# Windowed attention with its gradients: quads of four tiles below one another, merged stores, and x loads issued by GpSimd

## The chip, the cores and the metric

The kernel runs on one core of one Trainium2 chip. A core has five engines that run side by side and wait for one another by semaphores: TensorE (matmuls; PE in the profile, its weight loads PEld), VectorE (DVE), ScalarE (ACT), GpSimd (POOL) and SyncE (SP). Sixteen DMA engines move data between HBM and the on-chip memory (SBUF), and within SBUF; SyncE and GpSimd issue nearly all of those transfers here. TensorE writes its results to PSUM, which has eight banks. The metric is the device time of one execution in microseconds; lower is better.

## What is computed

The input x is an image of 256 x 256 pixels with 384 channels (bf16). It is cut into windows of 8 x 8 pixels, 1024 in all; each window is a sequence of 64 tokens. Within a window there is attention with one head, then an output projection. The kernel returns this output and, for a given grad_out, the gradients of x, wqkv and wo.

```python
xw = x in windows                                  # 1024 x 64 x 384
q, k, v = split(xw @ wqkv)
p = softmax(einsum('bqc,bkc->bqk', q, k) * C ** -0.5)
o = einsum('bqk,bkc->bqc', p, v) @ wo              # out_0, back in image order
out_1, out_2, out_3 = vjp of the above at (x, wqkv, wo), applied to grad_out
```

## The kernel before

**Products folded ahead.** Lines 61 to 107 load the weights once and make four 384 x 384 matrices of them, with wq, wk and wv the three column blocks of wqkv: A and its transpose AT from wq and wk with the scale in them, B and its transpose BT from wv and wo. So the loop never makes q, k and v. Per tile it makes y (x by A, L165) and z (grad_out by BT, L163), from which come scores and the gradients of p, and u = x B and v = x AT (L231).

**Tiles and quads.** A tile is 128 tokens: two windows, one below the other (16 image rows of 8 pixels); its lower 64 partitions (LO) hold one window, the upper 64 (HI) the other. A quad is four tiles. Before the change the four tiles of a quad lie side by side (`t0` to `t0 + 3` in the band `bp` of 16 rows, L349), so there are 128 quads.

**Steps.** The loop (L360) runs one step a quad, with three quads in work at once (L309): `a` (quad i+1) is projected, `b` (quad i) gets scores and softmax, `c` (quad i-1) gets its outputs. On each engine, instructions run in the order in which the program records them, without a scheduler (L353). A step on TensorE, in order: `sd` (scores of b, L177), u and v of b (L228 to L231), z of a (`project` kind 0, needs `dT`), a part of the weight gradient (`filler`, `pg`, every quad's share is summed later over groups of three quads), `attend` for tiles 0 and 1 of c, y of a (kind 1, needs `xT`), `filler`, `attend` for tiles 2 and 3 of c.

**What SyncE issues**, per step and in this order: `dT` and `xT` of quad i+2 (transposes of the loaded gradient and x, L130), `PS` of quad i (transpose of the probabilities and their gradient, L235, once VectorE's and ScalarE's parts of `ps` are done), four loads of x for quad i+3 (L120), and `tok` of quad i+1 (transposes y and z back to tokens, L169, once ScalarE has copied them out). Buffers: `xq` 10, `dq` 6, `xT` 3, `dT` 2, `PS` 2, `tok` 3.

**What GpSimd issues**: four loads of grad_out for quad i+3 (L121) between the stores of `attend` (L245). Its DMAs take turns on eight semaphores, and each waits until the DMA eight before it has landed.

**attend** (L247) works on a pair of tiles. For each tile it makes four results in a PSUM bank each: `po` (the output), `pu` and `pw` (for the weight gradients; VectorE copies them to `Uq` and `Wq`) and `pd` (the gradient of x; part of it comes from `tok`, in `token_part`). The pair uses all eight banks once. The matmuls are 64 x 64; in a "straight" one (`pu`, `pw`) a window stays in its half of the partitions, in a "crossed" one (`po`, `pd`) the window in LO comes out in HI and the other way round. ScalarE copies `po` and `pd` to SBUF (`keep`, L264); the pools for these copies have 8 buffers, two quads' worth for each output. As the halves are swapped, each copy leaves by two stores of 64 partitions (`store`, L243), so 16 stores a quad, 2048 in all.

Of the kernel before, what the change touches and what calls it, by code (L numbers as in the profile page):

```python
# [11 lines left out]
BF16 = mybir.dt.bfloat16  # L12
F32 = mybir.dt.float32

P = 128
WIN = 8
# [6 lines left out]
def kernel(  # L23
# [23 lines left out]
    CK = C // P  # L47
    J = 3 * C
    JK = J // P
    NBP = H // (2 * WIN)  # L50
    NT = W // WIN
    scale = float(C) ** -0.5

    const = ctx.enter_context(tc.tile_pool(name="const", bufs=1))
# [51 lines left out]
    GF_acc = const.tile([P, 2, CK, C], F32)  # L106
    nc.vector.memset(GF_acc[:], 0.0)

    def dram_tile(ap, bp, t):
        return ap[0, 2 * WIN * bp:2 * WIN * (bp + 1), WIN * t:WIN * (t + 1), :]  # L110

    LO, HI = slice(0, WT), slice(WT, P)
    OTHER = {0: HI, WT: LO}

    def load(st):
        bp, t0 = st["at"]
        st["xq"] = xq = grp.tile([P, QUAD, C], BF16, tag="xq", name="xq", bufs=2 * GQ + 4)
        st["dq"] = dq = qp.tile([P, QUAD, C], BF16, tag="dq", name="dq", bufs=6)
        for t in range(QUAD):
            nc.sync.dma_start(out=xq[:, t, :], in_=dram_tile(x, bp, t0 + t))  # L120
            nc.gpsimd.dma_start(out=dq[:, t, :], in_=dram_tile(grad_out, bp, t0 + t))  # L121

    def load_turn(st):
        xq, dq = st["xq"], st["dq"]
# [115 lines left out]
            return st["PS"][h, t, int((n == "ST") == (h == LO)), :]  # L240
        return st[n][h, t, :]

    def store(dst, src, bp, t):  # L243
        for h, w in ((LO, 1), (HI, 0)):
            nc.gpsimd.dma_start(out=dram_tile(dst, bp, t)[WIN * w:WIN * (w + 1)], in_=src[h, :])  # L245

    def attend(st, pair):  # L247
        bp, t0 = st["at"]
# [3 lines left out]
        def both(straight, crossed):  # L252
            for h, o, (dst, lhs, rhs, begin, done) in ((LO, LO, straight), (LO, HI, crossed), (HI, LO, crossed),
                                                       (HI, HI, straight)):
                nc.tensor.matmul(dst[o, :], lhsT=turned(st, lhs, t, h), rhs=st[rhs][h, t, :], start=begin, stop=done)  # L255

        def token_part(t, pd, first):
            for w, o in ((0, HI), (1, LO)):
                nc.tensor.matmul(pd[o, :], lhsT=st["ps"][:, t, w, :], rhs=st["tok"][:, :, t, w, :], start=first,  # L259
                                 stop=not first)  # L260

        def keep(name, eng, dst, t, src):
            sb = ob.tile([P, C], BF16, tag=name)
            ENG[EV[eng][t]](out=sb[:], in_=src[:])  # L264
            stores.append((dst, sb, bp, t0 + t))

        stores = []
        for t in pair:
            first = t == pair[0]
            po, pu = [ring.tile([P, C], F32, tag="r", name=n) for n in ("po", "pu")]  # L270
            if first:
                pd = ring.tile([P, C], F32, tag="r", name="pd")
                token_part(t, pd, True)
            both((pu, "ST", "xq", True, True), (po, "PT", "uq", True, True))
            keep("o", "o", out_0, t, po)
            ENG[EV["U"][t]](out=st["Uq"][:, t, :], in_=pu[:])  # L276
            pw = ring.tile([P, C], F32, tag="r", name="pw")
            if not first:
                pd = ring.tile([P, C], F32, tag="r", name="pd")
            both((pw, "Pb", "dq", True, True), (pd, "ST", "vq", not first, first))  # L280
            ENG[EV["W"][t]](out=st["Wq"][:, t, :], in_=pw[:])  # L281
            if not first:
                token_part(t, pd, False)
            keep("d", "d", out_1, t, pd)
        for s in stores:
            store(*s)

    fill = []

# [19 lines left out]
    def step(c, b, a, ahead):  # L309


        def on(st):
            return (lambda f, *r: f(st, *r)) if st is not None else (lambda f, *r: None)
        C_, B, A = on(c), on(b), on(a)
        B(scores)
        B(soft, 0)
        B(uv, 0, 0)
        B(uv, 0, 1)
        B(soft, 1)
        B(uv, 1, 0)  # L320
# [12 lines left out]
        B(soft, 5)  # L333
        B(turn)
        if ahead is not None:
            load(ahead)
        filler(1)
        C_(attend, (0, 1))
        split[0] = True
        for mo in range(CK):  # L340
            A(project, 1, mo)
        A(to_tokens)
        filler(1)
        split[0] = ALL
        C_(attend, (2, 3))

    G_ON_PE = 0
    EV = {"z": "AAA", "y": "AAA", "u": "AAAA", "v": "AAAA", "o": "AAAA", "U": "DDDD", "W": "DDDD", "d": "AAAA"}
    quads = [(bp, t0) for bp in range(NBP) for t0 in range(0, NT, QUAD)]  # L349
    sts = [{"at": q, "i": i} for i, q in enumerate(quads)]  # L350
    n = len(sts)
    AHEAD = 3
    with tc.manual_schedule(engines=MANUAL):  # L353
        for i in range(min(AHEAD, n)):
            load(sts[i])
            if i < AHEAD - 1:
                load_turn(sts[i])
        held = []
# [75 lines left out]
```

## Time and profile before

| what | value |
|---|---|
| median of 13 runs | 2037.19 us (2019.41 to 2047.17) |
| the profiled execution | 2047.17 us, of which the span of its instructions is 2045.1 us |
| TensorE clock granted | 0.995 of full speed |
| 2048 stores, GpSimd's time for one | 567 ns; 5.2 us to landing (median) |
| 512 loads of grad_out, GpSimd's time for one | 550 ns; 4.2 us to landing |
| 512 loads of x, SyncE's time for one (median) | 599 ns; 4.3 us to landing |
| transposes, SyncE's time (median): tok, xT, dT, PS | 5.64, 2.88, 2.02, 1.23 us |
| transposes to landing (median): tok, xT, dT, PS | 10.5, 6.6, 6.0, 4.9 us |
| 1024 copies of po and pd on ScalarE, mean of one | 490 and 500 ns |
| HBM read and written | 101.84 MB each, 100 GB/s over the span |

The profiled execution is the slowest of the 13 runs. In the profile, "L130 SPq DMA_TRANSPOSE" is SyncE issuing a transpose from line 130: the time shown is that for which the issue holds SyncE, not that of the transfer. An entry of the waits reads: engine, tile and line that waited, after the arrow what released it, then total us, number of times, longest. TensorE's matmuls overlap in the profile, so a busy share near 100% doesn't mean that it runs at its peak; how long a step takes is better read from the starts of a matmul that comes once a quad.

### The profile page before, as it was taken

What the parts mean: (1) busy time and instruction counts of PE and PEld (TensorE: products, weight loads), DVE (VectorE), ACT (ScalarE), POOL (GpSimd) and SP (SyncE); (2) the same over time, 40 slices, a digit from 0 to 9 for tenths busy, and PEclk for the clock granted to TensorE, in tenths of its full rate; (3) what the DMA queues carried; (4) which work ended last, traced back from release to release, by engine and by line L of the source; (5) the groups of instructions that cost most, each with busy time, mean ns of one, the idle gap of its engine ahead of it and who ended that gap; (6) DMA issues with size and microseconds to landing.
All of it is one profiled execution on the core that took longest, in us unless ns stands there. A gap on an engine that the chain in (4) does not pass through costs nothing.

```text
span 2045.1 us, 53141 instructions
## 1 busy us (share of the span) xinstructions
PE 1976.9 (97%) x19418; PEld 1125.2 (55%) x19418; DVE 1319.6 (65%) x2979; ACT 1423.0 (70%) x3213; POOL 1417.6 (69%) x2566
## 2 busy tenths in 40 slices
PE   8899999999999999999999999999999999999998
PEld 4455555555555555555555555555555555555555
DVE  5566666656666666666566666666666666666666
ACT  5677777767776766777667767767766767777674
POOL 3666777677766676766767767666776767777776
PEclk9899999999999999999999999999999999999999
DMA  9999999999999999999999999999999999999994
GB/s 201 184 212 208 213 216 209 207 206 209 214 212 200 213 211 215 214 209 202 205 216 212 216 215 214 211 213 205 217 209 202 217 208 219 213 220 213 215 219 115
DMA packets 1066854, 425.97 MB, mean 208 GB/s; under 512 B 950368, under 2 KB 1041248, under 8 KB 1066592
## 3 DMA queue, kind: packets, MB, share of 16 engines
q1 hardware_dynamic: 943312, 270.60, 81.3%
q0 software_dynamic: 122880, 151.68, 31.7%
q8 instruction: 152, 2.49, 0.5%
q14 instruction: 110, 0.90, 0.1%
q10 hardware_dynamic: 400, 0.29, 0.0%
HBM read 101.84 MB, written 101.84 MB: 100 GB/s over the span
## 4 chain that ended last, share of the span: by engine, by line
PE 78%; DMA 18%; ACT 2%; issue 0%; DVE 0%; SPq 0%; ACTq 0%; POOL 0%; POOLq 0%
PE pj L149 25%; PE pj L147 12%; PE pg L147 12%; DMA dT<-dq 11%; PE pg L149 10%; DMA PS<-ps 7%; PE pd L259 6%; PE pu L255 5%; PE sd L149 4%; PE pw L255 4%; ACT uq L231 1%; ACT vq L231 1%; PE pd L255 1%; DMA dq<-in_grad_out_dram 0%; DMA xT<-xq 0%
## 5 line engine op out<-in xcount | busy, mean ns | idle before, releaser
L245 POOL DMA_DIRECT2D out_dram<-sb x2048 | 1146.3, 567 | 549.7 <-DMA out_dram<-sb 225.0
L264 ACT CAST sb<-po 128x384 bf16<-128x384 f32 x512 | 250.9, 490 | 337.9 <-PE pu L255 312.2
L298 DVE TENSOR_TENSOR GF_acc<-pg,GF_acc 128x384 f32<-128x384 f32 x258 | 143.9, 558 | 519.4 <-PE pg L147 332.4
L149 PEld LDWEIGHTS <-xT 128*128 128x128 bf16 x3072 | 291.8, 98 | 182.2
L149 PE MATMUL pj<-B_sb,xT 128*128 128x384 bf16 x1536 | 333.4, 326 | 0.0
L149 PE MATMUL pj<-AT_sb,xT 128*128 128x384 bf16 x1536 | 333.3, 326 | 0.0
L121 POOL DMA_DIRECT2D dq<-in_grad_out_dram x512 | 274.1, 550 | 63.9 <-DMA out_dram<-sb 34.2
L149 PE MATMUL pj<-dT,BT_sb 128*128 128x512 bf16 x1152 | 275.5, 385 | 35.4 <-DMA dT<-dq 34.0
L276 DVE CAST Uq<-pu 128x384 bf16<-128x384 f32 x512 | 282.9, 552 | 38.5 <-PE pu L255 33.0
L231 ACT CAST uq<-pj 128x384 bf16<-128x384 f32 x512 | 247.4, 483 | 70.9 <-PE pj L149 67.8
L281 DVE CAST Wq<-pw 128x384 bf16<-128x384 f32 x512 | 280.2, 547 | 0.0
L147 PE MATMUL pj<-xT,A_sb 128*64 128x512 bf16 x2304 | 270.6, 380 | 1.0 <-DMA xT<-xq 1.0
L264 ACT CAST sb<-pd 128x384 bf16<-128x384 f32 x512 | 256.2, 500 | 0.7 <-PE pd L259 0.3
L231 ACT CAST vq<-pj 128x384 bf16<-128x384 f32 x512 | 250.1, 488 | 2.7 <-ACT uq L231 0.3
L165 ACT CAST yz<-pj 128x512 bf16<-128x512 f32 x384 | 224.2, 603 | 10.1 <-PE pj L147 2.1
L149 PEld LDWEIGHTS <-xq 128*128 128x128 bf16 x1572 | 154.4, 98 | 116.9 <-issue 3.7
L147 PEld LDWEIGHTS <-xq 128*64 128x64 bf16 x3000 | 170.3, 110 | 86.5
L163 ACT CAST yz<-pj 128x512 bf16<-128x512 f32 x384 | 207.2, 642 | 13.1 <-PE pj L149 11.7
L209 ACT COPY ps<-Pb 64x256 bf16<-64x256 bf16 x256 | 103.2, 403 | 149.7 <-DVE Pb L206 148.2
L149 PEld LDWEIGHTS <-BT_sb 128*128 128x128 bf16 x1152 | 109.2, 99 | 173.4 <-DMA dT<-dq 55.2
L255 PE MATMUL pu<-xq,PS 64*64 64x384 bf16 x1024 | 176.0, 336 | 17.2 <-DMA PS<-ps 17.0
L147 PEld LDWEIGHTS <-A_sb 128*64 128x64 bf16 x2304 | 134.3, 110 | 96.3 <-DMA xT<-xq 1.5
(60 smaller groups left out, 2486.9 us busy)
## 6 DMA issues: line engine op xcount, KB each, us to landing
out_dram<-sb POOLq DMA_DIRECT2D x2048, 48.0 KB, 5.2
xq<-in_x_dram SPq DMA_DIRECT2D x512, 96.0 KB, 4.3
dq<-in_grad_out_dram POOLq DMA_DIRECT2D x512, 96.0 KB, 4.2
dT<-dq SPq DMA_TRANSPOSE x128, 6.0
xT<-xq SPq DMA_TRANSPOSE x128, 6.6
tok<-yz SPq DMA_TRANSPOSE x128, 10.5
PS<-ps SPq DMA_TRANSPOSE x128, 4.9
w_sb<-in_wqkv_dram SPq DMA_DIRECT2D x1, 864.0 KB, 5.5
```

The lines of the kernel that those rows point to most:

```text
L121: nc.gpsimd.dma_start(out=dq[:, t, :], in_=dram_tile(grad_out, bp, t0 + t))
L147: nc.tensor.matmul(out[h], lhsT=lhsT[:, h], rhs=rhs, start=start, stop=stop)
L149: nc.tensor.matmul(out, lhsT=lhsT, rhs=rhs, start=start, stop=stop)
L163: ENG[EV["z"][mo]](out=yz[:, mo, :, 0:4:3, :], in_=pj[:])
L165: ENG[EV["y"][mo]](out=yz[:, mo, :, 1:3, :], in_=pj[:])
L231: cp(out=dst[:, t, :], in_=pj[:])
L245: nc.gpsimd.dma_start(out=dram_tile(dst, bp, t)[WIN * w:WIN * (w + 1)], in_=src[h, :])
L255: nc.tensor.matmul(dst[o, :], lhsT=turned(st, lhs, t, h), rhs=st[rhs][h, t, :], start=begin, stop=done)
L264: ENG[EV[eng][t]](out=sb[:], in_=src[:])
L276: ENG[EV["U"][t]](out=st["Uq"][:, t, :], in_=pu[:])
L281: ENG[EV["W"][t]](out=st["Wq"][:, t, :], in_=pw[:])
L298: nc.vector.tensor_tensor(out=GF_acc[:, f, ma, :], in0=pw[:], in1=GF_acc[:, f, ma, :], op=ALU.add)
```

## The change

A quad is now four tiles below one another: 64 image rows of one column of windows (`quads`, with `at` a row and a column; `windows` takes the place of `dram_tile`). The two tiles of a pair are then neighbours: the second window of the first tile borders on the first window of the second.

In `attend` the crossed results of the pair (`po`, `pd`) go to two banks by another rule. One bank ("outer" 0) takes the two windows that border on each other, the other ("outer" 1) the first window of the first tile and the second window of the second. Both are complete only when the second tile's matmuls are done, so ScalarE's four copies of a pair come after that, `po` first. Of each output, the inner bank's copy leaves by one store of 128 partitions and 16 image rows, the outer one's by two stores of 64 partitions: 12 stores a quad.

The x loads of the loop (quads 3 to 127) are issued by GpSimd, in turn with the loads of grad_out; SyncE keeps those of the first three quads. Below, SyncE's order in a step is `dT`, `xT`, `PS`, `tok`; GpSimd's is eight loads, six stores of one pair, six of the other.

```diff
-    def load(st):
-        bp, t0 = st["at"]
+    def windows(ap, st, first, count=2):
+        row, col = st["at"]
+        return ap[0, row + WIN * first:row + WIN * (first + count), col:col + WIN, :]
...
+    def load(st, queue):
...
-            nc.sync.dma_start(out=xq[:, t, :], in_=dram_tile(x, bp, t0 + t))
-            nc.gpsimd.dma_start(out=dq[:, t, :], in_=dram_tile(grad_out, bp, t0 + t))
+            queue.dma_start(out=xq[:, t, :], in_=windows(x, st, 2 * t))
+            nc.gpsimd.dma_start(out=dq[:, t, :], in_=windows(grad_out, st, 2 * t))
...
-    def store(dst, src, bp, t):
-        for h, w in ((LO, 1), (HI, 0)):
-            nc.gpsimd.dma_start(out=dram_tile(dst, bp, t)[WIN * w:WIN * (w + 1)], in_=src[h, :])
...
+        def both(straight, crossed, t, outer, **flags):
+            for h, o, (dst, lhs, rhs), fl in ((LO, LO, straight, {}), (LO, HI, crossed, flags), (HI, LO, crossed, flags),
+                                              (HI, HI, straight, {})):
+                at = dst if dst is not crossed[0] else dst[outer if h == LO else 1 - outer]
+                nc.tensor.matmul(at[o, :], lhsT=turned(st, lhs, t, h), rhs=st[rhs][h, t, :],
+                                 **{"start": True, "stop": True, **fl})
+
+        def token_part(t, pd, outer, **flags):
             for w, o in ((0, HI), (1, LO)):
...
+                nc.tensor.matmul(pd[outer if w == 0 else 1 - outer][o, :], lhsT=st["ps"][:, t, w, :],
+                                 rhs=st["tok"][:, :, t, w, :], **flags)
+
+        def keep(name, dst, src):
+            for outer in (0, 1):
+                sb = ob.tile([P, C], BF16, tag=name, name=name)
+                nc.scalar.copy(out=sb[:], in_=src[outer][:])
+                stores.append((dst, sb, outer))
+
+        t0, t1 = pair
         stores = []
...
+        pu = [bank("pu")]
+        po = [bank("po") for outer in (0, 1)]
+        pd = [bank("pd") for outer in (0, 1)]
+        token_part(t0, pd, 1, start=True, stop=False)
+        both((pu[0], "ST", "xq"), (po, "PT", "uq"), t0, 1)
+        nc.vector.tensor_copy(out=st["Uq"][:, t0, :], in_=pu[0][:])
+        pw = [bank("pw")]
+        both((pw[0], "Pb", "dq"), (pd, "ST", "vq"), t0, 1, start=False, stop=True)
+        nc.vector.tensor_copy(out=st["Wq"][:, t0, :], in_=pw[0][:])
+        pu.append(bank("pu"))
+        both((pu[1], "ST", "xq"), (po, "PT", "uq"), t1, 0)
+        keep("o", out_0, po)
+        nc.vector.tensor_copy(out=st["Uq"][:, t1, :], in_=pu[1][:])
+        pw.append(bank("pw"))
+        both((pw[1], "Pb", "dq"), (pd, "ST", "vq"), t1, 0, start=True, stop=False)
+        nc.vector.tensor_copy(out=st["Wq"][:, t1, :], in_=pw[1][:])
+        token_part(t1, pd, 0, start=False, stop=True)
+        keep("d", out_1, pd)
+        for dst, sb, outer in stores:
+            if outer:
+                nc.gpsimd.dma_start(out=windows(dst, st, 2 * t1 + 1, 1), in_=sb[LO, :])
+                nc.gpsimd.dma_start(out=windows(dst, st, 2 * t0, 1), in_=sb[HI, :])
+            else:
+                nc.gpsimd.dma_start(out=windows(dst, st, 2 * t0 + 1), in_=sb[:])
...
-            load(ahead)
+            load(ahead, nc.gpsimd)
...
-    quads = [(bp, t0) for bp in range(NBP) for t0 in range(0, NT, QUAD)]
+    quads = [(row, col) for row in range(0, H, 2 * WIN * QUAD) for col in range(0, W, WIN)]
...
-            load(sts[i])
+            load(sts[i], nc.sync)
```

More of the change, by code (lines that the diff above doesn't have):

```diff
@@ L49 @@
     JK = J // P
-    NBP = H // (2 * WIN)
-    NT = W // WIN
     scale = float(C) ** -0.5
@@ L107 @@
     nc.vector.memset(GF_acc[:], 0.0)
-    def dram_tile(ap, bp, t):
-        return ap[0, 2 * WIN * bp:2 * WIN * (bp + 1), WIN * t:WIN * (t + 1), :]
+    def windows(ap, st, first, count=2):
+        row, col = st["at"]
+        return ap[0, row + WIN * first:row + WIN * (first + count), col:col + WIN, :]
     LO, HI = slice(0, WT), slice(WT, P)
     OTHER = {0: HI, WT: LO}
-    def load(st):
-        bp, t0 = st["at"]
+    def load(st, queue):
         st["xq"] = xq = grp.tile([P, QUAD, C], BF16, tag="xq", name="xq", bufs=2 * GQ + 4)
@@ L241, in turned @@
         return st[n][h, t, :]
-    def store(dst, src, bp, t):
-        for h, w in ((LO, 1), (HI, 0)):
-            nc.gpsimd.dma_start(out=dram_tile(dst, bp, t)[WIN * w:WIN * (w + 1)], in_=src[h, :])
     def attend(st, pair):
-        bp, t0 = st["at"]
         if pair[0] == 0:
@@ L251, in attend @@
             st["Wq"] = grp.tile([P, QUAD, C], BF16, tag="Wq", name="Wq")
[L252 to L257, printed above, removed]
-            for w, o in ((0, HI), (1, LO)):
-                nc.tensor.matmul(pd[o, :], lhsT=st["ps"][:, t, w, :], rhs=st["tok"][:, :, t, w, :], start=first,
-                                 stop=not first)
@@ L262, in keep @@
[L262 to L265, printed above, removed]
-        stores = []
[L268 to L284, printed above, removed]
@@ L285, in attend, with bank @@
-        for s in stores:
-            store(*s)
+        def bank(name):
+            return ring.tile([P, C], F32, tag="r", name=name)
+        def both(straight, crossed, t, outer, **flags):
[4 more added lines that the diff above has]
+                                 **{"start": True, "stop": True, **fl})
```

## The prediction

> **What bounds the kernel now.** I read the page first (busy shares, DMA line, queues), then the waits of all engines, then SyncE's own timeline in two places, and last the times of single instructions and packets in the trace.
>
> The page says that two things are nearly always busy: TensorE and the DMA engines.
>
> ```profile
> PE 1976.9 (97%) x19418; PEld 1125.2 (55%) x19418; DVE 1319.6 (65%) x2979; ACT 1423.0 (70%) x3213; POOL 1417.6 (69%) x2566
> ...
> DMA  9999999999999999999999999999999999999994
> ...
> q1 hardware_dynamic: 943312, 270.60, 81.3%
> q0 software_dynamic: 122880, 151.68, 31.7%
> ```
>
> q1 is SyncE's queue (transposes and x loads), q0 GpSimd's (gradient loads and stores). Their packets overlap, so the shares may add up to over 100%; what the reader should take is that no slice has the DMA engines below nine tenths until the end.
>
> How often does TensorE wait? One quad begins with its first `sd` matmul; 128 such starts stand in the trace, from 22.0 to 2001.9 us. Of the 124 periods from the fourth on, 65 last under 15.2 us and most of these 15.12 or 15.13: that is TensorE's own pace, with nothing to wait for. The other 59 are longer, and everything above 15.13 adds up to 68 us. That, 3.3% of the span, is all a change around the DMAs can win. The waits say what is late:
>
> ```profile
> POOL out_dram L245 <- DMA out_dram<-sb: 225.0, 161, 4.0
> ...
> PEld L149 <- DMA dT<-dq: 55.2, 54, 5.2
> PE pj L149 <- DMA dT<-dq: 34.0, 35, 4.8
> ...
> PEld L255 <- DMA PS<-ps: 24.6, 33, 3.2
> ...
> PE pu L255 <- DMA PS<-ps: 17.0, 20, 3.0
> ```
>
> The matmul rows alone give 34.0 + 17.0 = 51 us, all behind transposes that SyncE issues. Why are they late, with two and three buffers each? SyncE's timeline in mid-run (start, time in us) answers:
>
> ```profile
> 1001.03 6.41 SPq L169 DMA_TRANSPOSE tok<-yz  x1
> 1007.67 1.47 SPq L130 DMA_TRANSPOSE dT<-dq  x1
> 1009.31 3.56 SPq L130 DMA_TRANSPOSE xT<-xq  x1
> 1013.04 1.21 SPq L235 DMA_TRANSPOSE PS<-ps  x1
> 1014.30 2.51 SPq L120 DMA_DIRECT2D xq<-in_x_dram  x4
> 1016.91 6.10 SPq L169 DMA_TRANSPOSE tok<-yz  x1
> ```
>
> One round is 15.9 us (1001.03 to 1016.91) and has no hole: SyncE goes from one issue to the next. It runs a whole quad behind: in the steps I sampled, `PS(i)` is issued 16 to 22 us after quad i's first `sd`, though its operand is there after about 8; TensorE tolerates up to about 18 to 20. Compare the start, when GpSimd issues no DMA yet:
>
> ```profile
> 24.06 2.51 SPq L120 DMA_DIRECT2D xq<-in_x_dram  x4
> 26.62 4.04 SPq L169 DMA_TRANSPOSE tok<-yz  x1
> 30.83 1.41 SPq L130 DMA_TRANSPOSE dT<-dq  x1
> 32.42 1.76 SPq L130 DMA_TRANSPOSE xT<-xq  x1
> 34.29 1.50 SPq L235 DMA_TRANSPOSE PS<-ps  x1
> 35.84 2.62 SPq L120 DMA_DIRECT2D xq<-in_x_dram  x4
> ```
>
> The same round takes 11.8 us here (24.06 to 35.84), the next one 14.0. So a transpose's issue lasts as long as the DMA engines need to take it: SyncE is held by the DMA engines, not by its own decoding. An x load costs SyncE 0.6 us in both places.
>
> GpSimd is as full. From its instruction times: 20 DMAs a quad at 0.55 to 0.57 us are 11.3 us; of the rest, 484 us in all (3.8 a quad) go by until the DMA eight before has landed, since its DMAs take turns on eight semaphores. Only 4 stores of 2048 found their copy by ScalarE unfinished.
>
> **What the Trainium skill says.** "DMA: Bandwidth & Descriptors", section "Issuing engines are not separate DMA queues": moving a DMA to another issuer saves only the sequencer's time, the same 16 engines run it. The trace agrees as far as it can: 8 rows of 768 B per engine and load cost 8 x 36 ns = 288 ns in q1 and 207 + 68 = 275 ns in q0 (medians of packets). Same page, "Why a DMA increments its semaphore by 16 and not by 1": a DMA spreads over the largest number up to 16 that divides the slowest dimension of both sides, while GpSimd's DMAs report from all 16. The trace agrees: a store of 8 x 8 x 384 puts data on 8 engines (16,384 packets each of 24 B and of 8 B are fillers for the others); a 16-row store should use all 16. Same page, "Queues, rings and completion order": an engine takes turns between queues packet by packet. The trace shows turns, but long ones: from 1237.5 to 1239 almost only transposes move, from 1240 to 1240.5 almost only GpSimd's packets.
>
> **The change part by part.**
> 1. *Quads of four tiles below one another.* A load still reads 16 rows of 8 pixels; counts and bytes stay. Rows of different tiles are no longer neighbours in HBM; at 100 GB/s of HBM traffic over the span I take 0, bound -0.1 to +0.2 us a quad.
> 2. *Merged stores.* Per pair and output three stores for four: 512 of 2048 go, 512 x 567 ns = 290 us less on GpSimd. Bytes stay; the fillers and reports of 1024 half stores go. Fillers and reports have 449.6 + 181.6 + 217.3 us of packet time on 16 engines; half of the fillers and a fifth of the reports are about 290 us, /16/128 = 0.14 us a quad.
> 3. *x loads to GpSimd.* 500 of 512 (the first three quads' stay). GpSimd: 500 x 550 ns = 275 us more, so 20 DMAs a quad as before. SyncE: 4 x 0.6 = 2.4 us less a quad. In GpSimd's order the loads stand before the first pair's stores; they are needed a full quad later, when `dT` and `xT` of that quad are issued.
> 4. *Crossed outputs in two banks.* The same matmuls in the same order, 8 banks a pair as before. ScalarE's first copy waits for the second tile: in the quad at 1727 the last `d` copy of a pair then ends about 0.35 us later. ScalarE sat idle 0.41 and 1.86 us ahead of the two pairs' first copies and 0.52 us before the next `uq`, so this is covered. The next banks are needed 0.5 to 1 us after they come free. Only the second tile's `pw` now takes the bank of the weight-gradient sum that `pd` took one matmul later: 0 to 0.05 us a quad. If the cover were gone, up to 0.35 us a pair.
>
> The sum is made in the DMA engines' time per quad, because both queues push back from there. Alone, SyncE's round is (11.8 + 14.0)/2 = 12.9 us, of which 2.5 are x: 10.4 remain. The mean round is 15.6 us, so 12 load-equivalents of GpSimd traffic (4 loads, 16 half stores) add 2.7 us, 0.22 each, partly because they slip in while SyncE spends 0.6 us on an x load that needs 0.29. Afterwards there are 16 load-equivalents at 0.22 (as now) to 0.29 us (nothing slips in): 10.4 + 3.5 to 4.6 = 13.9 to 15.0 us, less 0.14. That is under TensorE's 15.13, so TensorE becomes the limit. Not by much, and single rounds vary by 1 to 3 us [...], so I leave a third of the waits: 68 x 2/3 = 45 us gone. The profiled execution took 2047.2 us and is the longest of 13; TensorE's pace being fixed, the median of 2037.2 has about 10 us less of waits, 58. Two thirds of that is 38: **2000 us** (rounded). Its own range: all waits gone 1979, with a little spread 1976; waits down by a quarter 2022.
>
> **The rivals.**
> *A. DMA engines stay the limit.* If an x load costs 0.33 us in GpSimd's queue, a round is 10.4 + 16 x 0.33 = 15.7 and nothing moves. For: the DMA line has no hole. Against: 0.29 measured. Time 2034 (the fillers' share of the waits goes).
> *B. GpSimd becomes the limit (slower).* Place: its eight semaphores. All 20 DMAs of a quad pass through, so each delay of landing counts 20/8 = 2.5 times; 4 more of them are full loads, the bytes in flight rise by a third. Landing takes 5.2 us in the mean (over its 2560 DMAs) against about 3.4 for the fastest tenth; a third more of the 1.8 us spent queueing is 0.6, of which I take half, 0.3, since q1 loses what q0 gains. 2.5 x 0.3 = 0.75 us; GpSimd has some 0.8 us a quad of other idle time, of which I let half give way; 0.35 remain, x 127 = 44 us: 2080. It decides once the mean landing rises by over 0.2 us. For: GpSimd's 14 DMAs in a row (6 stores, 8 loads). Against: SyncE's freed time leaves the DMA engines open to it.
> *C. Late copies stall TensorE (slower).* 0.1 us on 256 pairs: 26 us on top of A, 2060. Against: the idle times above.
> *D. The change doesn't do what it says:* a merged store that cost twice on GpSimd would save nothing there. The gradient load, also 128 x 384, costs 550 ns, so no; it is within B.
>
> **How the numbers follow.** Main case 0.52 (all of it faster), A 0.17, B 0.25, C 0.06. A measurement here tells about 0.5% (10 us) from no change. A lies mostly within it (0.12), a little on either side. Faster 0.55, same 0.12, slower 0.33. The range reaches from 1976 over A and C to B's 2080, leaving out half of B and little else.
>
> **What would show it.** Right: SyncE has waiting time in every round and `PS` is issued about 8 to 12 us after the quad's `sd`; TensorE's waits for `dT` and `PS` fall below 20 us; most periods are 15.13. Wrong: GpSimd's waits for its own DMAs grow from 225, the landing of stores or loads rises above 5.5 us, and SyncE or ScalarE waits for them; or ScalarE's `po` copies appear as what TensorE waits for; or SyncE is still without a hole.

## The result, and the profile after

The changed kernel takes 2269.7 us in the median (11 runs, 2248.75 to 2294.28); the kernel before took 2038.4 us beside it. The ratio is 1.113 (95% interval 1.110 to 1.117): 231 us slower, where 2000 us were forecast and the range ended at 2080. The profiled execution of the changed kernel has a span of 2246.6 us.

The page of the changed kernel, the lines that answer to those shown of before (third and last: queue, packets, MB, share of 16 engines):

```profile
PE 2042.5 (91%) x19418; PEld 1195.0 (53%) x19418; DVE 1317.6 (59%) x2979; ACT 1415.8 (63%) x3213; POOL 1384.6 (62%) x2554
...
DMA  9999999999999999999999999999999999999995
...
q1 hardware_dynamic: 871312, 221.41, 69.2%
q0 software_dynamic: 122304, 200.57, 42.0%
```

TensorE's share falls from 97% to 91%. 49 MB went from q1 to q0 as intended, and the total is the same 426 MB. But the DMA line still shows nines: the engines are as busy as before and take longer over the same bytes (189 GB/s in the mean over the span, 208 before). The two shares times the span, over 128 quads, are the time that the packets took on 16 engines: 13.0 + 5.1 = 18.1 us a quad before, 12.1 + 7.4 = 19.5 now. (Packets of two queues overlap, which is why this is more than a quad lasts.) A quad now lasts 17.2 us in the mean, against 15.6, and TensorE's own pace is nearly what it was: the shortest quads take 15.20 us (15.13 before). So the loss is waiting. The waits of the changed kernel, TensorE's matmul rows:

```profile
PE pu L253 <- DMA PS<-ps: 115.6, 71, 4.9
...
PE pj L147 <- DMA dT<-dq: 64.6, 43, 4.8
```

These are the waits of before, for the same transposes, grown from 51 to 180 us on the matmul rows. What has changed is why the transposes are late. SyncE's queue of the changed kernel:

```profile
SPq L128 <- DMA dq<-in_grad_out_dram: 419.0, 131, 7.8
```

Before, this row read:

```profile
SPq L130 <- DMA dq<-in_grad_out_dram: 25.9, 14, 4.4
```

SyncE used to run without a hole, a quad behind; now it stands and waits for loads. Its timeline in mid-run (start, time in us):

```profile
998.05 6.23 SPq L167 DMA_TRANSPOSE tok<-yz  x1
1008.71 1.52 SPq L128 DMA_TRANSPOSE dT<-dq  x1
1010.40 3.45 SPq L128 DMA_TRANSPOSE xT<-xq  x1
1014.04 1.38 SPq L233 DMA_TRANSPOSE PS<-ps  x1
1015.53 6.43 SPq L167 DMA_TRANSPOSE tok<-yz  x1
1025.14 1.77 SPq L128 DMA_TRANSPOSE dT<-dq  x1
```

From 1004.28 (the end of `tok`) to 1008.71 SyncE does nothing, and again from 1021.96 to 1025.14. GpSimd's timeline over the first of these holes shows who it waits for (in brackets: idle time before the instruction, and the engine whose event the profile saw last):

```profile
999.24 0.52 POOL L119 DMA_DIRECT2D dq<-in_grad_out_dram  x1 [0.31 <-DMA out_dram<-d]
...
1003.17 0.56 POOL L290 DMA_DIRECT2D out_dram<-d  x1
1006.28 0.54 POOL L292 DMA_DIRECT2D out_dram<-o  x1 [2.55 <-ACT yz L163]
1009.12 0.56 POOL L289 DMA_DIRECT2D out_dram<-o  x1 [2.30 <-ACT o L264]
1009.67 0.56 POOL L290 DMA_DIRECT2D out_dram<-o  x1
```

The bracket names ScalarE, but these are GpSimd's own eight places: in the trace's semaphore events, the DMA eight before the store at 1006.28 landed at 1005.73, and the one eight before the store at 1009.12 is the gradient load of 999.24, which landed at 1008.57, after 9.3 us, beside the `tok` transpose. That one late load released both engines: SyncE's `dT` at 1008.71 and GpSimd's store at 1009.12. The second hole ends in the same way (the gradient load of 1017.00 landed at 1025.02; `dT` at 1025.14). These two are not exceptions: in 119 of the 128 rounds SyncE stands before `dT`, for 505 us in all (3.9 us a quad), and each of these holes ends with the landing of a gradient load of that quad. It is a loop of three: the loads that `dT` needs are the last of GpSimd's eight, they land late while `tok` runs, and while SyncE and GpSimd both wait for them, nothing new is given to the DMA engines: in quarter-microsecond steps of the trace, fewer than 12 packets were under way for about 0.9 us a quad (under 0.4 before). The mean landing of all GpSimd DMAs went from 5.19 to 5.98 us, and GpSimd's waits for the DMA eight before, worked out from the semaphore events, from some 510 to some 710 us.

### The profile page after: what moved, and what is told of

It is laid out like the page before. It is cut to its first block, busy times and chain, and to the rows that moved or that the text cites. A ratio compares the mean times of both kernels' runs of the same rounds, so it can differ in the third digit from the quotient of the medians.

```text
span 2246.6 us, 52492 instructions
## 1 busy us (share of the span) xinstructions
PE 2042.5 (91%) x19418; PEld 1195.0 (53%) x19418; DVE 1317.6 (59%) x2979; ACT 1415.8 (63%) x3213; POOL 1384.6 (62%) x2554
## 5 line engine op out<-in xcount | busy, mean ns | idle before, releaser
L264 ACT CAST o<-po 128x384 bf16<-128x384 f32 x512 | 220.4, 482 | 543.7 <-PE pu L253 520.3
L147 PE MATMUL pj<-dT,BT_sb 128*128 128x512 bf16 x1152 | 286.7, 397 | 72.8 <-DMA dT<-dq 64.6
L118 POOL DMA_DIRECT2D xq<-in_x_dram x500 | 271.6, 543 | 60.4 <-DMA out_dram<-o 33.8
L145 PE MATMUL pj<-xT,A_sb 128*64 128x512 bf16 x2304 | 305.4, 414 | 1.2 <-DMA xT<-xq 1.2
L289 POOL DMA_DIRECT2D out_dram<-o x256 | 147.3, 575 | 231.1 <-DMA dq<-in_grad_out_dram 113.5
L292 POOL DMA_DIRECT2D out_dram<-o x256 | 139.5, 545 | 216.0 <-DMA xq<-in_x_dram 57.7
L145 PEld LDWEIGHTS <-xq 128*64 128x64 bf16 x3000 | 206.6, 111 | 54.0 <-issue 3.4
L161 ACT CAST yz<-pj 128x512 bf16<-128x512 f32 x384 | 209.3, 636 | 36.8 <-issue 19.7
L163 ACT CAST yz<-pj 128x512 bf16<-128x512 f32 x384 | 209.8, 625 | 29.7 <-PE pj L145 28.7
L264 ACT CAST d<-pd 128x384 bf16<-128x384 f32 x512 | 225.5, 504 | 0.4 <-ACT o L264 0.2
L145 PEld LDWEIGHTS <-A_sb 128*64 128x64 bf16 x2304 | 165.1, 119 | 105.8 <-issue 30.8
L274 DVE CAST Uq<-pu 128x384 bf16<-128x384 f32 x256 | 141.4, 552 | 136.3 <-PE pu L253 134.4
```

What stands on the lines that cost most here:

```text
L118: queue.dma_start(out=xq[:, t, :], in_=windows(x, st, 2 * t))
L145: nc.tensor.matmul(out[h], lhsT=lhsT[:, h], rhs=rhs, start=start, stop=stop)
L147: nc.tensor.matmul(out, lhsT=lhsT, rhs=rhs, start=start, stop=stop)
L161: ENG[EV["z"][mo]](out=yz[:, mo, :, 0:4:3, :], in_=pj[:])
L163: ENG[EV["y"][mo]](out=yz[:, mo, :, 1:3, :], in_=pj[:])
L264: nc.scalar.copy(out=sb[:], in_=src[outer][:])
```

## The experiments

Ratios are to the kernel before, run on the same chip beside each; times can differ by some 10 us between chips, so runs on different chips are best compared by ratio. Two theories lead through all of them. W: GpSimd, with its eight places, is the limit; what counts is the number of its DMAs and how long each takes to land. C: the DMA engines themselves take longer when plain DMAs run beside the transposes. In SyncE's own queue x loads stand before or behind a transpose and hardly run beside one: in the trace of e1 (below) about a tenth of their bytes moved while packets of a transpose were under way, in that of e4, with x in a queue of its own, two thirds.

The table has all runs. "Beside" is what a quad moves in queues other than SyncE's, in units of one load (96 KB; whole stores count one, half stores a half). "Landing" is the mean over GpSimd's DMAs. "Places" is DMAs a quad x landing / mean period of a quad: how many of the eight are taken in the mean. "Packets" is the packet time of the queues per quad on 16 engines, as worked out above. Period, landing, places and packets come from the one profiled execution of each; for e2 and e15 that is the longest of its runs (2442 and 2035 us), for e10 one of 2196 us.

| kernel | GpSimd DMAs a quad | beside | time us | ratio (95%) | period | landing | places | packets |
|---|---|---|---|---|---|---|---|---|
| before | 20 | 12 | 2038 | 1 | 15.59 | 5.19 | 6.7 | 18.1 |
| changed | 20 | 16 | 2269.7 | 1.113 (1.110 to 1.117) | 17.17 | 5.98 | 6.9 | 19.5 |
| e3 vertical quads only | 20 | 12 | 2024.4 | 0.999 (0.996 to 1.001) | 15.33 | 5.12 | 6.7 | 18.0 |
| e1 x back on SyncE | 16 | 12 | 2004.8 | 0.988 (0.983 to 0.993) | 15.27 | 4.59 | 4.8 | 17.7 |
| e2 only x moved, stores as before | 24 | 16 | 2414.0 | 1.188 (1.180 to 1.196) | 18.68 | 5.21 | 6.7 | 19.5 |
| e4 x on ScalarE | 16 | 16 | 2128.9 | 1.050 (1.044 to 1.057) | 16.20 | 6.83 | 6.7 | 19.6 |
| e8 half of x on GpSimd | 18 | 14 | 1993.6 | 0.979 (0.975 to 0.983) | 15.17 | 5.32 | 6.3 | 18.0 |
| e13 three of four x on GpSimd | 19 | 15 | 2050.6 | 1.005 (1.003 to 1.007) | 15.65 | 5.65 | 6.8 | 18.2 |
| e11 x on GpSimd, half of gradient on SyncE | 18 | 14 | 1995.9 | 0.977 (0.972 to 0.982) | 15.19 | 5.25 | 6.2 | 17.9 |
| e12 half of x on ScalarE | 16 | 14 | 1995.1 | 0.977 (0.973 to 0.982) | 15.18 | 5.08 | 5.4 | 18.0 |
| e15 three of four x on ScalarE | 16 | 15 | 2017.3 | 0.994 (0.991 to 0.996) | 15.49 | 6.29 | 6.5 | 18.7 |
| e10 whole stores on ScalarE | 16 | 16 | 2195.7 | no interval (2158 to 2217) | 16.75 | 7.12 | 6.8 | 20.3 |
| e9 = e1 + four tiny DMAs | 20 | 12 | 2059.6 | 1.011 (1.005 to 1.017) | 15.72 | 5.24 | 6.7 | 18.4 |
| e14 = e8 + two tiny DMAs | 20 | 14 | 2053.2 | 1.015 (1.010 to 1.019) | 15.60 | 5.28 | 6.8 | 18.1 |
| e17 loads a quad earlier | 20 | 16 | 2286.9 | 1.128 (1.122 to 1.134) | 17.38 | 6.04 | 6.9 | 19.7 |
| e18 all loads on SyncE | 12 | 8 | 2342.9 | 1.151 (1.146 to 1.156) | 17.90 | 5.07 | 3.4 | 17.5 |
| e22 = e1, first U on ScalarE | 16 | 12 | 2003.5 | 0.984 (0.980 to 0.988) | 15.25 | 4.51 | 4.7 | 17.6 |
| e16 = e8, first U on ScalarE | 18 | 14 | 1983.4 | 0.980 (0.977 to 0.984) | 15.08 | 5.32 | 6.3 | 17.9 |

### Which part of the change: e1, e2, e3

e1 is the changed kernel with one word altered:

```diff
-            load(ahead, nc.gpsimd)
+            load(ahead, nc.sync)
```

> The changed kernel with the x loads of the loop back on SyncE: GpSimd has 16 DMAs a quad (4 loads, 4 whole and 8 half stores). Theory W (GpSimd's eight semaphores): GpSimd's round is 16 x 0.56 us plus at most 3 us of waiting for its own DMAs, so it limits nothing; SyncE is full again as in the kernel before; 2015 to 2050 us, mean landing of GpSimd's DMAs at or under 5.2 us. Theory H (vertical quads or the crossed banks cost the time): 2200 us or more, since both are still in.

e2 is the kernel before with only the x loads of the loop moved, and e3 the kernel before with only the quads turned (each with what follows from it at the places of use):

```diff
-            load(ahead)
+            load(ahead, nc.gpsimd)
...
-    quads = [(bp, t0) for bp in range(NBP) for t0 in range(0, NT, QUAD)]
+    quads = [(bp, col) for bp in range(0, NBP, QUAD) for col in range(NT)]
```

> The kernel before with nothing but its x loads of the loop moved to GpSimd: 24 DMAs a quad there. Theory W: each DMA counts, so it is clearly worse than the changed kernel, whose round of 17.2 us is 11.3 us of issue and 5.5 us of waiting: 24/20 of both is 20.2 us a quad, about 2600 us. Theory D (the x bytes cost more when they pass through GpSimd's queue, however many DMAs carry the rest): the same bytes are in that queue as in the changed kernel, so 2240 to 2300 us. Theory H: 2040 us, as neither vertical quads nor banks are in.

> The kernel before with only its quads made of tiles below one another; stores, banks and queues as before. Theories W and D: no difference, 2020 to 2055 us. Theory H in its HBM part: slower by over 3%, with longer landing of loads and stores.

e1 is some 10 us faster than W allowed and far from H's 2200; e2 lies between the numbers of W and D, so neither holds as it stands. Turning the quads is worth nothing (0.999), turning them and merging the stores 1.2% (0.988), and moving the x loads costs 12.7% on top of that (1.113/0.988), or 18.8% without the merge. The whole loss is the move. In e1 GpSimd has time to spare: its greatest wait is for stores whose copy isn't made yet.

```profile
POOL out_dram L292 <- ACT o L264: 689.2, 236, 28.1
```

In the changed kernel the same row has 45.5 us: there GpSimd is late for nearly all of them.

### Leaving SyncE's queue, and entering GpSimd's: e4

```diff
-            load(ahead, nc.gpsimd)
+            load(ahead, nc.scalar)
```

> The changed kernel with the x loads of the loop issued by ScalarE, on a third queue: SyncE is relieved as in the changed kernel, GpSimd has 16 DMAs a quad. Theory W: no full server is left; SyncE has holes, TensorE's waits for dT and PS fall under 20 us, 1985 to 2015 us (ScalarE has to issue 4 x 0.6 us a quad more and has the idle time for it). Theory D: only the passage through GpSimd's queue costs, so the same here. If the DMA engines themselves are the limit whatever the queue: 2030 us or more, with SyncE still full.

This misses W's number. GpSimd issues the 16 DMAs of e1, and still e4 is 6.3% slower than e1 (1.050/0.988). Nor has SyncE got the short round: its transposes alone hold it for 15.0 us a quad with hardly a hole, where in e1 they took 11.7 and the x loads 2.7. ScalarE's new work is a small part of the loss: TensorE waits 16 us for late copies of `o` (no such wait in e1), and the time rose by 124.

The changed kernel is a further 6.0% slower (1.113/1.050), but e4 is not a stop on the way to it. In the changed kernel SyncE's transposes take 12.7 us a quad, and SyncE stands for 3.9 us more, waiting for gradient loads (5 us in the whole of e4). Where e4's loss comes from is seen on the queue lines; e1's:

```profile
q1 hardware_dynamic: 943312, 270.60, 81.5%
q0 software_dynamic: 98304, 151.39, 31.4%
```

and e4's, with ScalarE's queue as q10:

```profile
q1 hardware_dynamic: 871312, 221.41, 71.8%
q0 software_dynamic: 98304, 151.39, 34.5%
q10 hardware_dynamic: 72400, 49.48, 11.9%
```

q0 moves the same 98,304 packets and 151.39 MB in both, but takes 31.4% of 2004.6 us in one and 34.5% of 2121.5 us in the other: 4.9 and 5.7 us a quad. The x loads' own 768-byte packets take 43.9 ns each in the mean in SyncE's queue and 61.3 ns in ScalarE's (medians 36 ns in both: it is the tail that grows), 1.4 and 1.9 us a quad. The transposes' packets go from 26.8 to 28.0 ns, 11.1 to 11.7 us a quad. So the four loads add 1.9 us of packet time a quad, of which only 0.5 is theirs; the rest is what all others lose beside them. The shares of e4 add up to 118%, so packets of different queues overlap, and a packet's time is not an engine's work alone; that the engines as a whole got slower is seen in the bytes, 212 GB/s over the span in e1 and 201 in e4. The mixing itself can be counted: at least three packets of transposes and three of loads or stores are under way for about 5.2 us a quad in e1, 9.7 in e4 and 7.9 in the changed kernel. Whether it matters that e4 has a third queue, e4 alone can't tell.

### The dose: e8 and e13 on GpSimd, e12 and e15 on ScalarE, e11

e8 moves two of a quad's four x loads, e13 three:

```diff
-            queue.dma_start(out=xq[:, t, :], in_=windows(x, st, 2 * t))
+            (queue if t < 2 else nc.sync).dma_start(out=xq[:, t, :], in_=windows(x, st, 2 * t))
```

For e13 it is `t < 3`; e12 and e15 are the same two edits with `load(ahead, nc.scalar)`. e11 leaves x where the change puts it and splits the other loads:

```diff
-            nc.gpsimd.dma_start(out=dq[:, t, :], in_=windows(grad_out, st, 2 * t))
+            (nc.gpsimd if t < 2 else nc.sync).dma_start(out=dq[:, t, :], in_=windows(grad_out, st, 2 * t))
```

> The changed kernel with the x loads of tiles 0 and 1 on GpSimd and those of tiles 2 and 3 on SyncE: half the dose, GpSimd issues 18 DMAs a quad (16 with x on SyncE: 2005 us; 20 in the changed kernel: 2270 us). Theory C (transposes and plain loads that run beside each other are slow together, whatever GpSimd has to spare): the loss goes with the loads that left SyncE's queue, so about half way, 2075 to 2150 us, with the mixed part of a quad between 4.8 and 7.8 us. Theory W (GpSimd's eight DMAs in flight become the limit only once its spare time, some 5.8 us a quad with x on SyncE, is used up): two more DMAs fit, 2000 to 2030 us.

The loss is not in proportion: half the dose (0.979) is faster than none (0.988), and a little faster than W's range. W, which asks whether GpSimd still has room, said so; C, as I had it, did not, since it let the mixed time grow with the loads moved: in e8 it is only 5.6 us a quad. For the next runs W was put into a number: GpSimd had 6.7 to 6.9 of its eight places taken in the runs in which it had no spare time, so that limit allows a landing of 15.2 x 8 x 0.84 / DMAs.

> The changed kernel with the x loads of tiles 0 to 2 on GpSimd and that of tile 3 on SyncE: 19 DMAs a quad on GpSimd, between 18 (1994 us) and 20 (2270 us). Theory W says that GpSimd, when it is the limit, keeps 83 to 86% of its eight places filled (DMAs a quad x mean landing / 8 / period, in the kernel before, in the changed one and in the three other runs where it had no spare time), so that a quad of 15.2 us allows a mean landing of 15.2 x 8 x 0.84 / DMAs: 6.4 us at 16, 5.7 at 18, 5.4 at 19, 5.1 at 20. Landing was 5.32 at 18, so at 19 it is just at its limit: some loss, 2005 to 2110 us, far less than three quarters of the way to 2270. A loss in proportion to the loads moved (theory C, which the run with half of them contradicts): 2200 us.

> The changed kernel, all x loads on GpSimd as there, but the gradient loads of tiles 2 and 3 on SyncE: 18 DMAs a quad on GpSimd and the same bytes in each queue as in the run with half of the x loads moved. Theory W (number and landing of GpSimd's DMAs, whatever they carry): like that run, 1985 to 2015 us. Theory T (it is x that arrives too late when it stands in GpSimd's order beside the gradient, or the transposes wait for both): the loss stays, above 2100 us.

> The changed kernel with the x loads of tiles 0 and 1 on ScalarE and those of tiles 2 and 3 on SyncE; GpSimd issues 16 DMAs a quad. With none on ScalarE: 2005 us, landing 4.59 us; with all four: 2129 us, 6.83 us. Theory W with its limit of 6.4 us at 16 DMAs: the landing stays under it, about 5.7, no loss, 1990 to 2020 us. In proportion to the loads that leave SyncE's queue (theory C): about 2065 us.

All three came out in W's range: e13 loses 2.6% to e8, with 6.8 places taken; e11, with all x loads on GpSimd and tiles 2 and 3 of the gradient on SyncE, is like e8, so it is not x as such that may not stand there. In e12, "in proportion" (2065 us) falls as well. But e12 and e8 also leave the engines with the same work beside the transposes, so these runs can't tell number from bytes.

### Number or bytes: e9, e14, e15

e9 and e14 add DMAs of 6 KB on GpSimd (four a quad to e1, two to e8), read from x into a tile that nothing reads:

```diff
+            ti = ob.tile([WIN, C], BF16, tag="ti", name="ti")
+            nc.gpsimd.dma_start(out=ti[:], in_=windows(x, st, 2 * t, 1)[0])
```

> The changed kernel with all x loads on SyncE and, in the places where the changed kernel issues x loads on GpSimd, four DMAs of 8 rows of 768 bytes there (6 KB each in place of 98 KB), into a tile that nothing reads. GpSimd issues 20 DMAs a quad as in the changed kernel, but the bytes in its queue are those of the kernel with x on SyncE. Theory W in its simplest form (the number of DMAs on GpSimd, each 0.56 us of issue and one of eight places): most of the loss returns, 2150 us or more. Theory C (bytes that run beside transposes): close to the kernel with x on SyncE, 2000 to 2035 us, landing below 5 us.

> The run with half of the x loads moved (tiles 0 and 1 on GpSimd, 2 and 3 on SyncE, 1994 us), and in the places of the other two on GpSimd a DMA of 6 KB each that nothing reads: 20 DMAs a quad on GpSimd as in the changed kernel, but 1376 KB a quad outside SyncE's queue in place of 1573. If the number of DMAs that pass through GpSimd's eight places decides (H1), most of the changed kernel's loss comes back: above 2150 us. If the bytes beside the transposes decide (H2), little comes back: 1995 to 2025 us. If both count, each with its own share, about what four tiny DMAs cost with x on SyncE (+46 us of four, from 2005): 2020 to 2060 us.

> The changed kernel with the x loads of tiles 0 to 2 on ScalarE and that of tile 3 on SyncE: 16 DMAs a quad on GpSimd, 1475 KB a quad outside SyncE's queue, as in the run with three of four on GpSimd (19 DMAs, 2051 us). With two of four on ScalarE 1995 us, with all four 2129. H2 (bytes beside the transposes decide): 2035 to 2065 us. H1 (GpSimd's places decide; 16 DMAs allow a landing of 6.4 us): no loss, 1995 to 2015 us.

e9 and e15 fall between the pure theories, and e14 into the range where both count. Put side by side as ratios to before, by GpSimd's DMAs and by what is beside the transposes, the runs say:

| beside, in loads | 16 DMAs | 18 or 19 | 20 DMAs |
|---|---|---|---|
| 12 | 0.988 (e1) | | 1.011 (e9) |
| 14 | 0.977 (e12) | 0.979 (e8), 0.977 (e11) | 1.015 (e14) |
| 15 | 0.994 (e15) | 1.005 (e13) | |
| 16 | 1.050 (e4) | | 1.113 (changed) |

Down a column is the price of bytes, along a row that of the number; but from the second row on the 16-DMA runs have ScalarE's queue as a third one. Without it, four more DMAs of next to no bytes cost 2.3% in the first row, two more cost 3.6% in the second (e14 against e8), and at 20 DMAs the bytes of two more loads cost 9.7%. With the third queue, the two loads cost 7.5%, of which 5.7 come with the last, and 16 against 20 DMAs is 6.0% in the last row. So both causes are there, each shown with the other held, and together they cost more (12.7% from e1 to the changed kernel) than e9's 2.3% and e4's 6.3%.

They act in different ways. The mixed time is about 5.2 us a quad in e1, 5.5 in e12, 8.2 in e15 and 9.7 in e4: nearly flat up to 14 loads' worth, then steep, like the times. e9 has no more of it than e1 (4.9). There GpSimd's waits for the DMA eight before go from some 100 us to over 500, and SyncE's transposes hold it for 12.2 us a quad instead of 11.7; which of the two costs the 2.3%, and why the transposes are slower, these runs don't settle. In e14 it is as in the changed kernel: SyncE stands 216 us, waiting for gradient loads.

Both begin late because TensorE covers them: up to 14 loads' worth and 18 DMAs a quad still fits into its 15.2 us. The first two loads that leave SyncE even bring 1% (e8, e11, e12 against e1), since SyncE's round gets shorter by 1.2 us and the waits for `dT` and `PS` all but vanish.

### Rate or lateness: e17. A third queue: e10

e17 issues all loads one quad earlier, with one more buffer for each:

```diff
-            step(get(i - 1), get(i), get(i + 1), get(i + AHEAD) if i >= 0 else None)
+            step(get(i - 1), get(i), get(i + 1), get(i + AHEAD + 1) if i >= 0 else None)
```

> The changed kernel with all its loads issued one quad earlier, with one more buffer each for x and the gradient; transposes stay where they were. If the loss is lateness alone, that is, loads that stand in GpSimd's order too near to the transposes that need them (theory T), SyncE no longer waits for dq and xq and the time falls to 1995 to 2040 us. If it is the rate (GpSimd and the engines cannot pass a quad's DMAs in 15.2 us, whenever they start), the lead is used up within a few quads and the time stays within 2% of 2270 us.

The lead buys nothing: 1.128, with SyncE's wait for the gradient at 406 us (419 before the edit). But TensorE no longer waits for the transposes (1.7 us for `dT`, 3.0 for `PS` on the matmul rows). It waits for ScalarE's copies, and these for the stores that have yet to empty their buffers:

```profile
ACT o L264 <- DMA out_dram<-o: 279.6, 152, 5.5
...
PE pj L145 <- ACT o L264: 144.9, 90, 4.5
```

With the loads put first, GpSimd falls behind with the stores. So it is the rate, not the distance between a load and its use. Spreading the eight loads among the stores, in place of issuing them in a row, was not tried.

e10 issues the whole stores (not the half ones) by ScalarE:

```diff
-                nc.gpsimd.dma_start(out=windows(dst, st, 2 * t0 + 1), in_=sb[:])
+                nc.scalar.dma_start(out=windows(dst, st, 2 * t0 + 1), in_=sb[:])
```

> The changed kernel with the four whole stores of a quad issued by ScalarE: x and gradient loads and the half stores stay on GpSimd, 16 DMAs a quad. Theory W: a mean landing of up to 6.4 us is allowed; if a third queue with 4 x 98 KB a quad lengthens the landings less than that, the loss is gone, 1995 to 2030 us. Theory Q3 (a third queue as such slows the transposes, as with x on ScalarE, whose landings grew to 6.8 us): 2090 to 2150 us, landing above 6.4. Theory T (x late because it stands on GpSimd): above 2150 us.

Four runs gave 2158 to 2217 us, a wider spread than the other kernels have; the fastest is 1.06 of before, not clearly slower than e4 (1.050) and faster than the changed kernel. GpSimd is back at 16 DMAs and all bytes beside the transposes are as in e4; in the profiled execution, of 2196 us, landing is 7.1 us, the packets take 20.3 us a quad and the mixed time is 10.4. All four lie above the ranges of W and Q3, and T, whose range they are in, is contradicted by e11 and e17. So a third queue does not take the loss away, but whether e10 loses more than e4, and by what, is left open.

### The other end: e18

```diff
-            nc.gpsimd.dma_start(out=dq[:, t, :], in_=windows(grad_out, st, 2 * t))
+            nc.sync.dma_start(out=dq[:, t, :], in_=windows(grad_out, st, 2 * t))
```

This is e1 with the gradient loads on SyncE too.

> The changed kernel with x loads and gradient loads all on SyncE, in the queue of the transposes; GpSimd is left with its 12 stores a quad. Theory C: still less runs beside transposes, so the mixed part of a quad falls below 4 us and the DMA engines do the same work in less time; but SyncE's own issue grows by 4 x 0.6 = 2.4 us a quad to 15.3 to 15.9 us a round and may itself become the limit: 2000 to 2080 us, never near 2270. Theory Q (SyncE's queue is the bottleneck and each load taken from it helps, each load added hurts; what the prediction rested on): slower than with x on SyncE by 4 x 0.6 x 127 = 305 us or more where SyncE had no slack, 2200 to 2310 us.

Here theory Q, that SyncE binds, is right but for 33 us above its range, and C's time is far off: 1.151. Nothing contends (packets 17.5 us a quad, the least of all; 3.4 places), but SyncE issues one after the other without a hole for 17.3 us a round:

```profile
1000.58 4.26 SPq L167 DMA_TRANSPOSE tok<-yz  x1
1005.03 3.20 SPq L128 DMA_TRANSPOSE dT<-dq  x1
1008.34 2.40 SPq L128 DMA_TRANSPOSE xT<-xq  x1
1010.84 1.39 SPq L233 DMA_TRANSPOSE PS<-ps  x1
1012.29 0.58 SPq L118 DMA_DIRECT2D xq<-in_x_dram  x1
1012.92 0.59 SPq L119 DMA_DIRECT2D dq<-in_grad_out_dram  x1
...
1017.92 6.02 SPq L167 DMA_TRANSPOSE tok<-yz  x1
```

Eight loads take it 5.6 us (1012.29 to 1017.92), in which the engines have little else to do: fewer than 12 packets are under way for 4.5 us a quad. So there is a best place between "all with the transposes" and "none": two to four of the eight loads on SyncE.

### TensorE's own pace, and the fastest kernel: e22, e16

After the change of banks the shortest quads take 15.20 us instead of 15.13. e22 is e1 with one copy a quad, that of the first pair, given to ScalarE:

```diff
-        nc.vector.tensor_copy(out=st["Uq"][:, t0, :], in_=pu[0][:])
+        (nc.scalar.copy if t0 == 0 else nc.vector.tensor_copy)(out=st["Uq"][:, t0, :], in_=pu[0][:])
```

> The changed kernel with x loads on SyncE, and the copy of the first tile's pu out of its bank made by ScalarE in place of VectorE, where it stands behind the sum of the weight gradients. If this late copy is what lifts TensorE's own pace from 15.13 to 15.20 us a quad after the change of banks, the shortest periods fall to 15.13 to 15.15 us and the time by 127 x 0.06 = 8 us, to about 1997 us. If the banks' order as such is the cause, the shortest periods stay at 15.20; if ScalarE lacks the time, its later copies hold TensorE and the time rises above 2010 us.

The shortest quads are back at 15.13 us, and 108 of the 124 from the fourth on take just that; the time against e1 is within the intervals (0.984 and 0.988). e16 is e8 with this copy given to ScalarE in both pairs of a quad:

> The run with half of the x loads moved, and the first tile's pu copied by ScalarE in place of VectorE, which by itself brought TensorE's own pace from 15.20 to 15.13 us a quad. With half of x moved nearly every quad runs at that pace, so the two add up: 127 x 0.07 = 9 us from 1994, 1983 to 1990 us, ratio to the kernel before 0.974 to 0.978.

e16 takes 1983.4 us (1978.65 to 1988.03), 0.980 (0.977 to 0.984) of before and by the ratios 12% less than the changed kernel. Its times lie below all of e8's (1992.21 to 1996.58), but the two ran on different chips and their ratios don't differ, so the last 10 us are shown by the trace rather than by the ratio: 121 of the 124 quads from the fourth on take 15.13 us, where 122 of e8's take 15.20. Its page and its waits for `PS`, the longest that it has for a transpose in the loop:

```profile
PE 1959.1 (99%) x19418; PEld 1124.3 (57%) x19418; DVE 1209.6 (61%) x2723; ACT 1502.0 (76%) x3469; POOL 1253.7 (63%) x2304
```

```profile
PEld L253 <- DMA PS<-ps: 3.3, 1, 3.3
PE pu L253 <- DMA PS<-ps: 3.1, 1, 3.1
```

The waits of 51 us for `dT` and `PS` that the prediction set out to win are down to 3.5. TensorE alone binds now.

## Why the prediction was wrong

**The step that failed** is the sum in the third part, "16 load-equivalents at 0.22 (as now) to 0.29 us", with "the same 16 engines run it" behind it: that a load costs the engines the same in whichever queue it stands. The prediction drew this from the Trainium skill, "DMA: Bandwidth & Descriptors", section "Issuing engines are not separate DMA queues": transfers of all issuers run on the same 16 engines and interleave, and a second issuer saves only sequencer time. The section doesn't say what the interleaving costs, and the runs show that it does cost: four loads a quad, moved from SyncE's queue to ScalarE's with GpSimd left alone, made the kernel 6.3% slower. The 0.29 us were 8 rows by the median packet, 36 ns. The mean packet was 46 ns before, so a load took 0.37 us of the engines even there; in ScalarE's queue it takes 0.49, and the four slow their neighbours by 1.4 us a quad more. In GpSimd's queue a load took 0.39 us by mean packets before and takes 0.44 after, where the prediction had 0.275 by medians. In the changed kernel the packets take 1.4 us a quad more than before, where by the sum they should have stayed as they were or fallen.

**"10.4 remain"** for SyncE's transposes alone was too low. It came from two rounds at the start, when GpSimd issued nothing. Beside GpSimd's traffic the transposes' issue took 12.0 us a quad before, and 12.7 after the x loads had gone: SyncE was relieved of 2.5 us of x loads, lost 0.7 of it to slower transposes and then stood 3.9 us a quad, waiting for gradient loads. The sum has no term for that wait: 12.7 + 3.9 = 16.6 us of the 17.2 that a quad takes, against the 13.9 to 15.0 forecast.

**Rival B** was right in place and sign, and wrong in size. It said that GpSimd's eight places would bind and that each delay of landing counts 2.5 times. Landing rose by 0.79 us: 0.79 x 2.5 x 127 = 251 us, and 231 were measured. That the two are so near is in part luck: e4 loses 124 us against e1 without a DMA more on GpSimd. Rival B had set the rise at 0.3, as half of "a third more of the 1.8 us spent queueing", on the argument that SyncE's freed time leaves the engines open. It also let GpSimd's other idle time give way; that grew, from about 105 to about 130 us. Its point of decision, a landing over 0.2 us longer, was passed four times over. The profile of before had the sign of it: GpSimd was already full, with 6.7 of its places taken, and the change put larger DMAs through the same places.

**Part by part.** The turned quads: 0 forecast, 0.999 measured. The merged stores: 290 us less on GpSimd and 0.14 us a quad of fillers forecast; POOL's busy time fell by 295 us from before to e1, and q0's packet time by 0.14 us a quad from e3 to e1. GpSimd's own price for an x load, 550 ns forecast, is 543 in the trace. The banks: 0 to 0.05 us a quad forecast with ScalarE's cover in view; it is 0.07, and e22 shows that it comes from VectorE, whose copy of the first `pu` stands behind the sum of the weight gradients. Rival C (late copies) has no part in the loss: in the changed kernel TensorE waits for ScalarE under 10 us in all, and never for a copy of `o` or `d`. Rival A, that a load costs the engines more than 0.29 us in GpSimd's queue, was right in kind, but it set the load at 0.33 us and forecast no loss. Rival D is excluded by e1 and by the 49 MB in q0.

**What would show it wrong** named what happened: GpSimd's waits for its own DMAs (some 510 to some 710 us), landing above 5.5 us (5.98), and SyncE waiting for them (419 us). One sign of being right came too: SyncE has waiting time in nearly every round; but it is spent on late loads.

## What to carry to other kernels

Before a DMA is moved to another issuer, count two things for each queue: how many of its places are taken (DMAs a period x landing / period; the runs at TensorE's pace had at most 6.3 of GpSimd's eight, those in which GpSimd had nothing to spare 6.7 to 6.9), and how much will run beside the transposes that didn't before. Moving all four x loads cost 12.7% where moving two of four gained 1%: try half before all, and look for the cliff, since TensorE's longer work covered the first part of the price here. Take the cost of a transfer from mean packet times and at full traffic, not from medians or from the quiet start.

## What the runs showed of the hardware

- A DMA's price depended on what stood in the other queues: the same 98,304 packets of GpSimd's queue took 4.9 us a quad with x on SyncE, 4.8 with half of x on ScalarE, 5.4 with three quarters and 5.7 with all of it there. The mixed time goes the same way (5.2, 5.5, 8.2 and 9.7 us a quad), and of the packets' times it is the tail that grows (the x loads' 768-byte packets keep a median of 36 to 39 ns). What slows mixed packets inside the engines is not settled by these runs.
- Four DMAs of 6 KB a quad, 2% of the bytes of GpSimd's queue, cost 2.3% (e9): the number of DMAs had a price apart from their size.
- A transpose's issue holds SyncE for longer, the slower the engines are to take it: `tok` 4.8 us in e1, 5.8 in e4, 6.3 in the changed kernel (medians), for the same bytes.
